# Retention then SwiGLU FFN on one core: FFN of the first chunk begun on two batches, with one more weight block loaded before the fourth batch

## The chip, the cores and the metric

The kernel runs on one core of a Trainium2 chip. The metric is the device time in microseconds from one launch to its end. The times of the kernel before are a median of 237.69 us over 7 runs, from 237.36 to 238.91. Five engines matter: TensorE (PE), VectorE (DVE), ScalarE (ACT), GpSimd (POOL) and the DMA queues, of which GpSimd issues most transfers and SyncE (SP) the first and the last.

## The reference

Inputs are q, k, v of shape (4 batches, 8 heads, 768 positions, 64), two FFN weights of 512 x 1536, one of 1536 x 512, and a gain vector. The first half is a recurrent retention per batch and head, the second an FFN over all 3072 tokens of width 512 (8 heads of 64):

```python
state = gamma[None, :, None, None] * state + np.einsum('bhd,bhe->bhde', k[:, :, t], v[:, :, t])
y[:, :, t] = scale * np.einsum('bhd,bhde->bhe', q[:, :, t], state)
...
xn = x / rms * rms_g
g = xn @ w_gate
silu = g * (1.0 / (1.0 + np.exp(-g)))
val = xn @ w_val
return (silu * val @ w_out)
```

## The kernel before, in words

The 768 positions are cut into six chunks of 128. A *group* is one chunk of all four batches, 512 token columns. For each group there is an attention part, batch by batch, and an FFN part over the 512 columns together. The recurrence is turned into matmuls within a chunk (scores with a decay mask) and a running state per batch between chunks.

The attention part is written as pieces, each named by a letter in the lists of the code. `piece_c` casts batch 0's first loads to bf16. `piece_v` (V) scales v by the decay into vp, on VectorE for batches 0 to 2 of chunk 0 and otherwise on GpSimd. `piece_t` (T) transposes q and k on TensorE for chunks 0 and 1, eight 128-wide matmuls and one ScalarE copy to qkT; for later chunks it issues DMA transposes from SyncE. `piece_a` (A) computes the scores, eight matmuls on 64 rows, and masks them with two VectorE multiplies into am. `piece_y` (Y) computes y, in chunks after the first also the part from the state and kv for the state's update, and ends with ScalarE's sum of squares (xsq). `piece_rstd` (R) makes the reciprocal root on GpSimd. `piece_n` (N) scales y to xn on VectorE. `piece_x` (X) transposes xn on TensorE and evicts it to the batch's 128 columns of xnT: for batches 0 and 1 of chunk 0 by four ScalarE activations, else by one VectorE multiply. `piece_s` and `piece_sb` (S) make the state of chunk 0: four matmuls, one ScalarE copy, two GpSimd casts.

The FFN part of a group has 12 blocks of 128 hidden units. Block n is `gv(n)` (L332 on): four matmuls for the gate (g_ps), four for the value (v_ps), each with the group's columns as the moving side, then silu on ScalarE (sg) and one multiply on VectorE (hT). The down projection follows: in group 0 in twelve pieces of four matmuls (three thirds of the hidden units by four batches), in later groups batch by batch. PSUM has two pools of four buffers, one for the FFN (fps) and one for attention (aps); Y of chunk 0 takes its buffer from the FFN's pool.

The order of all work is written out by hand, since the tile framework runs in manual order. Each engine takes its instructions strictly as they are written. The prologue is the string in L405 and L406: letters with a batch number, H with a count for warm-up matmuls of 256 columns on zeros, G and U for one piece of gate and value weights. After it the main loop (L426 on) goes through the *slots* of a group: each slot is one FFN block or one down piece, followed by pieces of the next chunk's attention, placed by PLAN1 for chunk 1 and PLAN for later ones, and by loads and early pieces for the chunk after that (AHEAD0, AHEAD, LATE0; L is a load of q, k and v, W one of w_out). In group 0, slots 0 to 3 use columns of three batches only (`gv_first`), X of batch 3 stands in slot 1, and the fourth batch's columns of these four blocks follow in slot 3, packed as 128-wide matmuls into one PSUM bank.

All loads by GpSimd go through one queue in the order of issue. The framework turns over eight semaphores for them, so that each issue waits for the landing of the eighth before it, and the instructions behind it on GpSimd wait too. In the prologue the order is q, k, v of batches 1 to 3, then three pairs of weight pieces: 384, 384 and 768 hidden units (WB, L142).

Of the kernel before, what the change touches and what calls it, by code (L numbers as in the profile page):

```python
# [9 lines left out]
F32 = mybir.dt.float32  # L10
BF16 = mybir.dt.bfloat16
# [6 lines left out]
def kernel(  # L18
# [11 lines left out]
    nc = tc.nc  # L30
    ctx.enter_context(tc.manual_schedule())

    B, H, S, D = q.shape
    C = 128
# [27 lines left out]
            nc.sync.dma_start(out=x, in_=src[0].rearrange("h (c p) d -> c p h d", p=C)[0])  # L62
            raw[name] = x

    def load(c, b):
        d = cur.setdefault((c, b), {})
        for name, src in (("qb", q), ("kb", k)):
            x = work.tile([128, DM], BF16, name=name, bufs=8)
            nc.gpsimd.dma_start(  # L69
                out=x.rearrange("p (h d) -> p h d", h=H),  # L70
                in_=src[b].rearrange("h (c p) d -> c p h d", p=C)[c])
            d[name] = x
        d["v_f"] = loads.tile([128, H, D], F32, name="v_f")
        nc.gpsimd.dma_start(out=d["v_f"], in_=v[b].rearrange("h (c p) d -> c p h d", p=C)[c])  # L74

    cur = {}
    load_first()
# [42 lines left out]
    nc.vector.memset(mhalf, -0.5)  # L120
    ident = const.tile([128, 128], BF16, name="ident")
    make_identity(nc, ident)
    for b in range(1, B):
        load(0, b)

    g_bc = const.tile([128, DM], F32, name="g_bc")
# [12 lines left out]
    wg_v = moe_w_gate.rearrange("(k p) n -> p k n", p=128)  # L139
    wv_v = moe_w_val.rearrange("(k p) n -> p k n", p=128)  # L140
    wo_v = moe_w_out.rearrange("(n p) m -> p n m", p=128)
    WB = ((0, 384), (384, 768), (768, DFF))  # L142

    def load_wg(i):
        sl = slice(*WB[i])
        nc.gpsimd.dma_start(out=wg_b[:, :, sl], in_=wg_v[:, :, sl])

    def load_wv(i):
        sl = slice(*WB[i])
        nc.gpsimd.dma_start(out=wv_b[:, :, sl], in_=wv_v[:, :, sl])  # L150
# [65 lines left out]

    def piece_y(c, b):
        d = cur[c, b]
        pool, tag = (fps, "ff") if c == 0 else (aps, "at")
        y_ps = pool.tile([128, H, D], F32, name="y_ps", tag=tag)  # L220
        first = True
        for hp in range(NHP):
            for i in range(2):
                h = 2 * hp + i
                last = c == 0 and h == H - 1
                nc.tensor.matmul(y_ps[:, h, :], d["am"][:, i, hp, :], d["vp"][:, h, :],  # L226
                                 start=first, stop=last, skip_group_check=True)
                first = False
        if c > 0:
            for hp in range(NHP):  # L230
                nc.tensor.matmul(y_ps[:, 2 * hp:2 * hp + 2, :], d["qT"][:, hp, :], st_b[b][:, hp, :],  # L231
                                 start=False, stop=hp == NHP - 1, skip_group_check=True)
        if 0 < c < NCH - 1:
            kv_ps = piece_kv(c, b)
        x = y_ps if c == 0 else work.tile([128, H, D], F32, name="x", bufs=5)
        if c > 0:
            nc.vector.tensor_tensor(  # L237
                out=x, in0=y_ps, in1=ydec[:, c, :, None].to_broadcast([128, H, D]), op=ALU.mult)
        xsq = work.tile([128, DM], F32, name="xsq", bufs=1)
        ssq = work.tile([128, 1], F32, name="ssq")  # L240
        nc.scalar.activation(xsq, x.rearrange("p h d -> p (h d)"), AF.Square,  # L241
                             accum_out=ssq)
        d["ssq"] = ssq
        d["x"] = x
        if c == 0:
            return
        piece_rstd(c, b)
        if c < NCH - 1:
            nc.vector.tensor_tensor(out=st_f[b], in0=st_f[b], in1=kv_ps, op=ALU.add)
            piece_sb(b)  # L250

    def piece_kv(c, b):
        d = cur[c, b]
        kv_ps = aps.tile([128, NHP, 128], F32, name="kv_ps", tag="at")
        for hp in range(NHP):
            sl = slice(hp * 128, (hp + 1) * 128)
            nc.tensor.matmul(kv_ps[:, hp, :], d["kb"][:, sl],  # L257
                             d["vp"][:, 2 * hp:2 * hp + 2, :], start=True, stop=True)
        return kv_ps

    def piece_s(b):
        nc.scalar.copy(st_f[b], piece_kv(0, b))

    def piece_sb(b):
        for i in range(2):
            r = slice(i * 64, i * 64 + 64)
            nc.gpsimd.tensor_copy(st_b[b][r, :, i * 64:i * 64 + 64], st_f[b][r, :, i * 64:i * 64 + 64])  # L267
# [21 lines left out]
    def piece_x(c, b):  # L289
        d = cur[c, b] if c == 0 else cur.pop((c, b))  # L290
        if c > 1:
            return
        xn = d["xn"]
        xt_ps = aps.tile([128, KS, 128], BF16, name="xt_ps", tag="at")
        for s in range(KS):
            nc.tensor.transpose(xt_ps[:, s, :], xn[:, s * 128:(s + 1) * 128], ident)  # L296
        xnT = cur[c, "xnT"][:, :, b * C:(b + 1) * C]
        if c == 0 and b < 2:
            for s in range(KS):
                nc.scalar.activation(xnT[:, s, :], xt_ps[:, s, :], AF.Copy, scale=g_col[:, s:s + 1])  # L300
            return
        nc.vector.tensor_tensor(
            out=xnT, in0=xt_ps,
            in1=g_col[:, :, None].to_broadcast([128, KS, 128]), op=ALU.mult)
# [5 lines left out]

    PLAN = dict(a=(5, 5, 9, 9), y=(7, 8, 11, 12), n=(9, 10, 13, 13))

    PLAN1 = dict(v=(7, 9, 11, 14), t=(8, 10, 12, 15), a=(9, 11, 14, 17), y=(10, 13, 16, 19), n=(12, 15, 18, 21), x=(13, 17, 20, 22))

    def attention(c):
        s = [[] for _ in range(24 if c == 1 else 16)]
        s[0].append(lambda: begin(c))
        plan = PLAN1 if c == 1 else PLAN
        pieces = dict(v=piece_v, t=piece_t, a=piece_a, y=piece_y, n=piece_n, x=piece_x)
        for b in range(B):  # L320
            for n, slot in plan.items():
                s[slot[b]].append(lambda f=pieces[n], b=b: f(c, b))
        return s


    def ffn(c):
# [5 lines left out]
        def gv(n0, n1=None, t=slice(0, GT)):  # L332
            n1 = n0 + 1 if n1 is None else n1
            w = t.stop - t.start
            g_ps = fps.tile([128, n1 - n0, w], F32, name="g_ps", tag="ff")
            v_ps = fps.tile([128, n1 - n0, w], F32, name="v_ps", tag="ff")
            for ps, w_b in ((g_ps, wg_b), (v_ps, wv_b)):
                for n in range(n0, n1):
                    for s in range(KS):
                        nc.tensor.matmul(ps[:, n - n0, :], w_b[:, s, n * 128:(n + 1) * 128], xnT[:, s, t],  # L340
                                         start=s == 0, stop=s == KS - 1)
            sg = ffw.tile([128, n1 - n0, w], BF16, name="sg")
            nc.scalar.activation(sg, g_ps, AF.Silu)  # L343
            nc.vector.tensor_tensor(out=hT[:, n0:n1, t], in0=sg, in1=v_ps, op=ALU.mult)  # L344


        EARLY = 4
        early = slice(0, GT - C)

        def gv_first(n):  # L350
            gv(n, t=early)
            if n == 1:
                piece_x(0, B - 1)
            if n == EARLY - 1:
                gv(0, EARLY, slice(GT - C, GT))

        o_t = {}

# [22 lines left out]
            nc.sync.dma_start(out=out_v[c, b], in_=o_sb)  # L381

        for n in range(NFF):
            slots.append(lambda n=n: gv_first(n) if c == 0 and n < EARLY else gv(n))
        if c == 0:
            for i in range(3):
                for b in range(B):
# [11 lines left out]
    def warm_up(c, n):  # L399
        for i in range(n):  # L400
            nc.tensor.matmul(hot_ps, hot[:, 0:128], hot, start=True, stop=True)  # L401

    P = dict(C=lambda c, b: piece_c(b), V=piece_v, T=piece_t, A=piece_a, Y=piece_y,
             R=piece_rstd, N=piece_n, X=piece_x, G=lambda c, i: load_wg(i), U=lambda c, i: load_wv(i), H=warm_up)
    for step in ("H9 H8 C0 T0 H4 V0 A0 H4 V1 T1 H4 G0 Y0 R0 U0 H4 A1 V2 T2 H4 Y1 R1 G1 U1 H2 A2 N0 T3 Y2 R2 "  # L405
                 "X0 N1 H2 A3 X1 N2 H9 H6 X2 H3 V3 Y3 H6 G2 U2 R3 N3").split():  # L406
        P[step[0]](0, int(step[1]))
    make_causal()
    load(1, 0)

    L, T, V, W = load, piece_t, piece_v, lambda c, i: load_wo(i)
    AHEAD = {1: ((L, 0),), 3: ((L, 1),), 5: ((L, 2),), 7: ((T, 0),), 8: ((T, 1),), 9: ((L, 3),), 11: ((T, 2),),
             13: ((V, 0),), 14: ((V, 1), (T, 3)), 15: ((V, 2), (V, 3))}


    AHEAD0 = {2: ((L, -1, 1),), 4: ((W, 0),), 5: ((L, -1, 2),), 6: ((W, 1),), 8: ((L, -1, 3),), 9: ((W, 2), (L, 0)),
              11: ((L, 1),), 13: ((T, 0),), 14: ((L, 2),), 15: ((T, 1),), 19: ((T, 2), (L, 3))}
    LATE0 = {0: ((V, 0), (V, 1), (V, 2)), 1: ((T, 3),), 4: ((V, 3),)}

    def ahead(c, i):  # L420
# [5 lines left out]
    for c in range(NCH):  # L426
        f_slots = ffn(c)
        a_slots = attention(c + 1) if c + 1 < NCH else [[] for _ in range(16)]
        for i, f_slot in enumerate(f_slots):
            if i == NFF + 1 and c > 0:  # L430

                for f in a_slots[i]:
                    f()
                a_slots[i] = []
            f_slot()
            if c == 0 and i < B:
                piece_s(i)
                piece_sb(i)
            for f in a_slots[i]:
                f()  # L440
            ahead(c, i)
            if c == 0 and i == 22:
                nc.sync.dma_start(out=g_bc, in_=moe_rms_g.partition_broadcast(128))
# [28 lines left out]
```

## Time and profile before

| What | Value |
|---|---|
| median of 7 runs | 237.69 us |
| the profiled execution | 237.69 us |
| its span, first to last instruction | 236.0 us |
| TensorE busy | 226.5 us |
| VectorE, ScalarE, GpSimd busy | 126.8, 88.9, 128.6 us |
| first FFN matmul starts at | 20.29 us |
| first down matmul starts at | 45.02 us |
| first FFN matmul of group 1 starts at | 61.53 us |
| landing of k and v of batch 3, chunk 0 | 14.63, 15.76 us |
| landing of the weight pairs (gate, value) | 17.25, 19.89; 21.81, 23.73; 27.48, 31.45 us |

In the lines of the profile, L and a number is the line of the kernel, then come engine, operation and the tiles written and read. In the timeline the first two columns are start and duration in us; in the chain of work too. Square brackets give the idle time before an instruction and what ended it. TensorE's matmuls overlap and their ends are modelled, so the distance from start to start is the better measure of one. Letters with a number (Y3, X2) stand for a piece and a batch; for chunk 1 a 1 stands in front (A11 is A of batch 1 in chunk 1).

### The profile page before, as it was taken

The numbers are of one execution on the slowest core, as the hardware profiler recorded it, in microseconds if no ns is written. First come the engines' busy times: TensorE is split into PE (matmuls) and PEld (weight loads), VectorE is DVE, ScalarE is ACT, GpSimd is POOL, SyncE is SP. The second block draws the span as 40 slices with busy tenths as digits, with TensorE's granted clock in tenths as the row PEclk, the third lists the DMA queues.
The fourth block names the chain that finished last, engine by engine and source line by source line (L and its number), as shares of the span: only waits on it lengthen the run. The fifth ranks groups of instructions, "written<-read, shape, count | busy, mean of one in ns | idle before, by whom it ended". The sixth has DMA issues, their size and how long they took to land.

```text
span 236.0 us, 4231 instructions
## 1 busy us (share of the span) xinstructions
PE 226.5 (96%) x1587; PEld 119.3 (51%) x1613; DVE 126.8 (54%) x212; ACT 88.9 (38%) x172; POOL 128.6 (55%) x198
## 2 busy tenths in 40 slices
PE   7979999999899999999999999999999999999994
PEld 4657744565345555445554445554445554444443
DVE  6585435678347794147794147794148582243300
ACT  7475534432433433333433333433332532433221
POOL 8978989987997458970559970559300202000000
PEclk9999999999999999999999999999999999999999
DMA  8999999999999999999698999295900025200022
GB/s 140 176 191 205 211 192 205 208 194 130 190 278 178 116 161 158 178 188 99 94 128 120 171 215 141 34 132 136 181 0 0 3 44 150 75 0 0 0 89 90
DMA packets 87956, 30.69 MB, mean 130 GB/s; under 512 B 78528, under 2 KB 83392, under 8 KB 87936
## 3 DMA queue, kind: packets, MB, share of 16 engines
q0 software_dynamic: 54432, 16.78, 74.5%
q1 hardware_dynamic: 32832, 13.51, 29.7%
q8 instruction: 12, 0.20, 0.4%
q10 hardware_dynamic: 672, 0.13, 0.3%
q14 instruction: 8, 0.07, 0.1%
HBM read 28.58 MB, written 6.29 MB: 148 GB/s over the span
## 4 chain that ended last, share of the span: by engine, by line
PE 85%; DVE 4%; ACT 4%; POOL 3%; issue 2%; ACTq 0%; DVEq 0%; POOLq 0%
PE g_ps L340 26%; PE v_ps L340 26%; PE o_ps L375 21%; PE a_ps L208 3%; PE y_ps L226 2%; PE hot_ps L401 2%; PE y_ps L231 2%; PE kv_ps L257 2%; DVE am L214 1%; DVE xn L286 1%; PE o_ps L365 1%; ACT xsq L241 1%; DVE x L237 1%; PE xt_ps L296 1%; POOL rstd L274 1%
## 5 line engine op out<-in xcount | busy, mean ns | idle before, releaser
L344 DVE TENSOR_TENSOR hT<-sg,v_ps 128x512 bf16<-128x512 bf16 (+1 forms) x73 | 49.5, 678 | 80.0 <-PE v_ps L340 70.1
L340 PE MATMUL v_ps<-xnT,wv_b 128*128 128x512 bf16 (+2 forms) x298 | 73.5, 368 | 0.4
L340 PE MATMUL g_ps<-xnT,wg_b 128*128 128x512 bf16 (+2 forms) x293 | 73.2, 368 | 0.5
L343 ACT ACTIVATE sg<-g_ps 128x512 bf16<-128x512 f32 (+1 forms) x73 | 43.0, 589 | 64.9 <-PE g_ps L340 62.5
L375 PE MATMUL o_ps<-wo_b,hT 128*128 128x512 bf16 x267 | 61.9, 379 | 0.5 <-issue 0.2
L340 PEld LDWEIGHTS <-wv_b 128*128 128x128 bf16 x304 | 29.1, 98 | 33.1
L340 PEld LDWEIGHTS <-wg_b 128*128 128x128 bf16 x304 | 27.7, 98 | 29.4 <-issue 0.4
L375 PEld LDWEIGHTS <-hT 128*128 128x128 bf16 x276 | 26.2, 98 | 28.7 <-DVE hT L344 0.2
L271 POOL TENSOR_SCALAR ms<-ssq 128x1 f32<-128x1 f32 x24 | 5.6, 232 | 62.2 <-ACT xsq L241 62.0
L241 ACT ACTIVATE xsq<-x 128x512 f32<-128x512 f32 x20 | 12.6, 630 | 35.1 <-DVE x L237 33.3
L214 DVE TENSOR_TENSOR am<-a_ps,causal 128x512 bf16<-128x512 f32 x40 | 24.9, 679 | 0.0
L380 ACT COPY o_sb<-o_ps 128x512 f32<-128x512 f32 x23 | 13.2, 582 | 29.3 <-PE o_ps L375 23.3
L69 POOL DMA_DIRECT2D qb<-in_q_dram x23 | 21.9, 950 | 0.3 <-issue 0.2
L175 POOL TENSOR_TENSOR vp<-v_f,vdec 128x512 bf16<-128x512 f32 x21 | 21.5, 1041 | 0.5
L74 POOL DMA_DIRECT2D v_f<-in_v_dram x23 | 21.3, 925 | 0.1
L69 POOL DMA_DIRECT2D kb<-in_k_dram x23 | 20.8, 902 | 0.0
L267 POOL CAST st_b<-st_f 64x256 bf16<-64x256 f32 x40 | 18.1, 454 | 1.3
L237 DVE TENSOR_TENSOR x<-y_ps,ydec 128x512 f32<-128x512 f32 x20 | 13.7, 684 | 2.9 <-PE y_ps L231 2.9
L282 DVE SCALAR_TENSOR_TENSOR xn<-x,rstd,g_bc 128x512 bf16<-128x512 f32 x16 | 12.7, 791 | 3.5 <-POOL rstd L274 3.5
L274 POOL TENSOR_TENSOR rstd<-ms,mhalf 128x1 f32<-128x1 f32 x24 | 13.3, 555 | 2.0
L401 PE MATMUL hot_ps<-hot 128*128 128x256 bf16 x65 | 11.6, 329 | 1.1 <-DVE hot L93 1.1
L226 PEld LDWEIGHTS <-am 128*128 128x128 bf16 x192 | 8.8, 98 | 5.3 <-DVE am L214 0.9
(71 smaller groups left out, 145.3 us busy)
## 6 DMA issues: line engine op xcount, KB each, us to landing
v_f<-in_v_dram POOLq DMA_DIRECT2D x23, 256.0 KB, 7.5
out_dram<-o_sb SPq DMA_DIRECT2D x23, 256.0 KB, 2.4
qb<-in_q_dram POOLq DMA_DIRECT2D x23, 128.0 KB, 6.0
kb<-in_k_dram POOLq DMA_DIRECT2D x23, 128.0 KB, 7.1
wo_b<-in_moe_w_out_dram POOLq DMA_DIRECT2D x3, 512.0 KB, 9.6
wg_b<-in_moe_w_gate_dram POOLq DMA_DIRECT2D x2, 384.0 KB, 6.5
wv_b<-in_moe_w_val_dram POOLq DMA_DIRECT2D x2, 384.0 KB, 7.6
wg_b<-in_moe_w_gate_dram POOLq DMA_DIRECT2D x1, 768.0 KB, 8.9
```

The source lines that it names most:

```text
L69: nc.gpsimd.dma_start(out=x.rearrange("p (h d) -> p h d", h=H), in_=src[b].rearrange("h (c p) d -> c p h d", p=C)[c])
L74: nc.gpsimd.dma_start(out=d["v_f"], in_=v[b].rearrange("h (c p) d -> c p h d", p=C)[c])
L175: (nc.vector if c == 0 and b < 3 else nc.gpsimd).tensor_tensor(out=d["vp"], in0=d["v_f"], in1=vdec[:, c, :, None].to_broadcast([128, H, D] ...
L214: nc.vector.tensor_tensor(out=am[:, i], in0=a_ps[i], in1=mask, op=ALU.mult)
L237: nc.vector.tensor_tensor(out=x, in0=y_ps, in1=ydec[:, c, :, None].to_broadcast([128, H, D]), op=ALU.mult)
L267: nc.gpsimd.tensor_copy(st_b[b][r, :, i * 64:i * 64 + 64], st_f[b][r, :, i * 64:i * 64 + 64])
L274: nc.gpsimd.tensor_tensor(out=rstd, in0=ms, in1=mhalf, op=ALU.pow)
L340: nc.tensor.matmul(ps[:, n - n0, :], w_b[:, s, n * 128:(n + 1) * 128], xnT[:, s, t], start=s == 0, stop=s == KS - 1)
L343: nc.scalar.activation(sg, g_ps, AF.Silu)
L344: nc.vector.tensor_tensor(out=hT[:, n0:n1, t], in0=sg, in1=v_ps, op=ALU.mult)
L375: nc.tensor.matmul(o_ps, hT[:, n, b * C:(b + 1) * C], wo_b[:, n, :], start=n == 0, stop=n == NFF - 1)
L401: nc.tensor.matmul(hot_ps, hot[:, 0:128], hot, start=True, stop=True)
```

## The change

The weights' first dimension of the hidden units is cut into four equal pieces of 384. The prologue issues the first two pairs of weight pieces before the loads of q, k, v of batch 3, which are now issued one by one, and the other two pairs behind them. T, A, Y, R, N and X of batch 3, and X of batch 2, leave the prologue; V of batch 3 goes to GpSimd behind the first load of chunk 1. Batch 1's X is evicted by VectorE.

Group 0's first twelve slots are `first(i)`: slot 0 has blocks 0 and 1 on two batches together, X of batch 2, block 2 on two batches, and the third batch's columns of blocks 0 to 2 packed. Slots 1 to 7 have blocks 3 to 9 on three batches, each followed by pieces of the fourth batch and the states. Slots 8 to 10 have the fourth batch's columns of blocks 0 to 9, packed, then come blocks 10 and 11 on all columns. Group 1 begins with blocks 0 and 1 on three batches (`second`), with X of chunk 1's batch 3 between them. PLAN1 is shifted by one or two slots, and the loads of AHEAD0 with it; the first two loads of chunk 2 are both issued in slot 10.

```diff
-    WB = ((0, 384), (384, 768), (768, DFF))
+    WB = tuple((i * 384, (i + 1) * 384) for i in range(4))
...
-        pool, tag = (fps, "ff") if c == 0 else (aps, "at")
+        pool, tag = (fps, "ff") if c == 0 and b < B - 1 else (aps, "at")
...
-        if c == 0 and b < 2:
+        if (c, b) == (0, 0):
             for s in range(KS):
                 nc.scalar.activation(xnT[:, s, :], xt_ps[:, s, :], AF.Copy, scale=g_col[:, s:s + 1])
...
-    PLAN1 = dict(v=(7, 9, 11, 14), t=(8, 10, 12, 15), a=(9, 11, 14, 17), y=(10, 13, 16, 19), n=(12, 15, 18, 21), x=(13, 17, 20, 22))
+    PLAN1 = dict(v=(9, 10, 13, 16), t=(9, 11, 13, 16), a=(10, 12, 15, 18), y=(11, 14, 17, 20),
+                 n=(13, 16, 19, 22), x=(15, 18, 21, None))
...
-        def gv_first(n):
-            gv(n, t=early)
-            if n == 1:
-                piece_x(0, B - 1)
-            if n == EARLY - 1:
-                gv(0, EARLY, slice(GT - C, GT))
+        def first(i):
+            two, three, third, fourth = slice(0, 2 * C), slice(0, 3 * C), slice(2 * C, 3 * C), slice(3 * C, GT)
+            if i == 0:
+                gv(0, 2, two)
+                piece_x(0, 2)
+                gv(2, 3, two)
+                gv(0, 3, third)
+            elif i < 8:
+                gv(i + 2, t=three)
+            else:
+                gv(*((0, 4), (4, 8), (8, 10), (11, 12))[i - 8], fourth if i < 11 else slice(0, GT))
+                if i == 10:
+                    gv(10)
+            for f, *x in {1: ((piece_s, 0),), 2: ((piece_t, 0, 3), (piece_s, 1)), 3: ((piece_a, 0, 3),),
+                          4: ((piece_y, 0, 3), (piece_rstd, 0, 3), (piece_s, 2)), 5: ((piece_n, 0, 3), (piece_s, 3)),
+                          7: ((piece_x, 0, 3),)}.get(i, ()):
+                f(*x)
+
+        def second(n):
+            gv(n, t=slice(0, GT - C))
+            if n == 0:
+                piece_x(1, B - 1)
+            else:
+                gv(0, 2, slice(GT - C, GT))
...
-    for step in ("H9 H8 C0 T0 H4 V0 A0 H4 V1 T1 H4 G0 Y0 R0 U0 H4 A1 V2 T2 H4 Y1 R1 G1 U1 H2 A2 N0 T3 Y2 R2 "
-                 "X0 N1 H2 A3 X1 N2 H9 H6 X2 H3 V3 Y3 H6 G2 U2 R3 N3").split():
+    for step in ("H9 H8 C0 T0 H4 V0 A0 H4 V1 T1 H4 G0 U0 Y0 G1 U1 R0 H4 A1 V2 T2 H4 q3 Y1 R1 k3 H2 A2 H6 N0 Y2 R2 v3 "
+                 "H2 X0 N1 H3 X1 N2 H6 G2 U2 G3 U3").split():
...
-    AHEAD0 = {2: ((L, -1, 1),), 4: ((W, 0),), 5: ((L, -1, 2),), 6: ((W, 1),), 8: ((L, -1, 3),), 9: ((W, 2), (L, 0)),
-              11: ((L, 1),), 13: ((T, 0),), 14: ((L, 2),), 15: ((T, 1),), 19: ((T, 2), (L, 3))}
+    AHEAD0 = {3: ((L, -1, 1),), 5: ((W, 0),), 6: ((L, -1, 2),), 8: ((W, 1),), 9: ((L, -1, 3),),
+              10: ((W, 2), (L, 0), (L, 1)), 13: ((T, 0),), 15: ((T, 1),), 16: ((L, 2),), 20: ((L, 3),), 23: ((T, 2),)}
```

More of the change, by code (lines that the diff above doesn't have):

```diff
@@ L63, in load_first, with load @@
             raw[name] = x
-    def load(c, b):
+    def load(c, b, parts="qkv"):
         d = cur.setdefault((c, b), {})
[L67 to L74, printed above, removed]
+        for n in parts:
+            if n == "v":
+                x = d["v_f"] = loads.tile([128, H, D], F32, name="v_f")
+            else:
+                d[n + "b"] = work.tile([128, DM], BF16, name=n + "b", bufs=8)
+                x = d[n + "b"].rearrange("p (h d) -> p h d", h=H)
+            nc.gpsimd.dma_start(out=x, in_=dict(q=q, k=k, v=v)[n][b].rearrange("h (c p) d -> c p h d", p=C)[c])
     cur = {}
@@ L122 @@
     make_identity(nc, ident)
-    for b in range(1, B):
+    for b in (1, 2):
         load(0, b)
@@ L262, in piece_s @@
         nc.scalar.copy(st_f[b], piece_kv(0, b))
+        piece_sb(b)
     def piece_sb(b):
@@ L321, in attention @@
             for n, slot in plan.items():
-                s[slot[b]].append(lambda f=pieces[n], b=b: f(c, b))
+                if slot[b] is not None:
+                    s[slot[b]].append(lambda f=pieces[n], b=b: f(c, b))
         return s
@@ L344, in gv @@
             nc.vector.tensor_tensor(out=hT[:, n0:n1, t], in0=sg, in1=v_ps, op=ALU.mult)
-        EARLY = 4
-        early = slice(0, GT - C)
-        def gv_first(n):
-            gv(n, t=early)
-            if n == 1:
-                piece_x(0, B - 1)
-            if n == EARLY - 1:
-                gv(0, EARLY, slice(GT - C, GT))
+        def first(i):
[19 more added lines that the diff above has]
+                piece_x(1, B - 1)
+            else:
+                gv(0, 2, slice(GT - C, GT))
         o_t = {}
@@ L383, in ffn @@
         for n in range(NFF):
-            slots.append(lambda n=n: gv_first(n) if c == 0 and n < EARLY else gv(n))
+            slots.append(lambda n=n: first(n) if c == 0 else second(n) if c == 1 and n < 2 else gv(n))
         if c == 0:
@@ L403 @@
     P = dict(C=lambda c, b: piece_c(b), V=piece_v, T=piece_t, A=piece_a, Y=piece_y,
-             R=piece_rstd, N=piece_n, X=piece_x, G=lambda c, i: load_wg(i), U=lambda c, i: load_wv(i), H=warm_up)
-    for step in ("H9 H8 C0 T0 H4 V0 A0 H4 V1 T1 H4 G0 Y0 R0 U0 H4 A1 V2 T2 H4 Y1 R1 G1 U1 H2 A2 N0 T3 Y2 R2 "
-                 "X0 N1 H2 A3 X1 N2 H9 H6 X2 H3 V3 Y3 H6 G2 U2 R3 N3").split():
+             R=piece_rstd, N=piece_n, X=piece_x, G=lambda c, i: load_wg(i), U=lambda c, i: load_wv(i), H=warm_up,
+             **{n: lambda c, b, n=n: load(c, b, n) for n in "qkv"})
+    for step in ("H9 H8 C0 T0 H4 V0 A0 H4 V1 T1 H4 G0 U0 Y0 G1 U1 R0 H4 A1 V2 T2 H4 q3 Y1 R1 k3 H2 A2 H6 N0 Y2 R2 v3 "
+                 "H2 X0 N1 H3 X1 N2 H6 G2 U2 G3 U3").split():
         P[step[0]](0, int(step[1]))
@@ L409 @@
     load(1, 0)
+    piece_v(0, 3)
     L, T, V, W = load, piece_t, piece_v, lambda c, i: load_wo(i)
@@ L435 @@
             f_slot()
-            if c == 0 and i < B:
-                piece_s(i)
-                piece_sb(i)
             for f in a_slots[i]:
```

## The prediction

> **What bounds the kernel now.** I read the page first, then the chain that ended last, then the timeline by stretches. The page says that TensorE is busy almost throughout and holds most of that chain.
>
> ```profile
> PE 226.5 (96%) x1587; PEld 119.3 (51%) x1613; DVE 126.8 (54%) x212; ACT 88.9 (38%) x172; POOL 128.6 (55%) x198
> ...
> PE 85%; DVE 4%; ACT 4%; POOL 3%; issue 2%; ACTq 0%; DVEq 0%; POOLq 0%
> ```
>
> So time is won in two ways only: useful matmuls begin earlier, or TensorE waits less. It runs its list in order, so one late operand holds everything behind it. The timeline shows where useful work begins:
>
> ```profile
> 18.04 0.74 DVE L286 TENSOR_SCALAR xn<-y_ps,rstd 128x512 bf16<-128x512 f32 x1
> ...
> 19.28 0.69 DVE L302 TENSOR_TENSOR xnT<-xt_ps,g_col 128x512 bf16<-128x512 bf16 x1 [0.49 <-PE xt_ps L296]
> ...
> 19.63 0.82 PE L401 MATMUL hot_ps<-hot 128*128 128x256 bf16 x6
> ...
> 20.29 0.81 PE L340 MATMUL g_ps<-xnT,wg_b 128*128 128x384 bf16 x4
> ```
>
> The first FFN matmul waits for the third batch's columns (19.97), then for six warm-up matmuls. From there to group 1 TensorE waits, reckoned from start to start of its matmuls, about 1.9 us in all: 0.34 us (of a 0.44 us gap), 0.30 and 0.21 around the attention pieces, and 1.04 us at batch 3's last transpose, 59.31 to 60.35. After 66 us I find no wait worth a name.
>
> Two more stretches supply durations. First, a transpose followed by its eviction, with an hT multiply ahead of it on VectorE:
>
> ```profile
> 23.11 0.39 PE L296 MATMUL xt_ps<-ident,xn 128*128 128x128 bf16 x4
> ...
> 23.38 0.55 DVE L344 TENSOR_TENSOR hT<-sg,v_ps 128x384 bf16<-128x384 bf16 x1 [0.61 <-PE v_ps L340]
> 23.86 0.68 DVE L302 TENSOR_TENSOR xnT<-xt_ps,g_col 128x512 bf16<-128x512 bf16 x1
> ...
> 26.38 1.06 PE L340 MATMUL g_ps<-xnT,wg_b 128*128 128x128 bf16 x16
> 27.28 1.06 PE L340 MATMUL v_ps<-xnT,wv_b 128*128 128x128 bf16 x16
> ```
>
> From the transpose's start to usable columns it is 24.54 - 23.11 = 1.43 us. Second, in the chain of work, the chain from one batch's y to the next batch's scores:
>
> ```profile
> 42.32 0.61 DVE x L237
> ...
> 43.01 0.59 ACT xsq L241
> ...
> 43.64 0.99 ACT qkT L198
> ```
>
> y began at 41.36 and the scores at 44.69, so 3.33 us.
>
> **The change, part by part.** Prices on TensorE, from start to start in these rows: four 384-wide matmuls 0.65, four 512-wide 0.86, a 256-wide 0.109, a 128-wide 0.056 (16 in 0.90). VectorE follows the last matmul's issue by 0.27 us, ScalarE by 0.20; on VectorE starts lie 0.60 apart for 512 elements, 0.47 for 384.
>
> *Start.* Batch 3's T and A leave the prologue, and batch 1's columns go from ScalarE to VectorE. Up to batch 2's scores (13.42) nothing differs. VectorE then ends am at 15.14, xn0 at 15.80, xn1 at 16.46 as before; batch 1's transposes start at 16.52, and its columns are ready 0.22 + 0.22 + 0.69 later, at 17.65. ScalarE, free of the 1.01 us qkT copy, ends batch 0's four columns near 17.4. The first FFN matmul comes at 17.7 in place of 20.29: **-2.6 us**. Weights: v2 landed at 12.87, and a 384-column piece takes 1.9 us of the stream (21.81 to 23.73), so the first pair lands near 14.8 and 17.0, needed at 17.7 and 18.6.
>
> *Moved work.* T (0.45), A (0.42), Y (0.22) of batch 3 and X (0.22) of batch 2, once under the waits of the prologue, now stand between FFN blocks: **+1.3**.
>
> *Narrow blocks.* Columns stay the same, matmuls become more: group 0 was 32x0.1625 + 32x0.056 + 64x0.216 = 20.8 and becomes 24x0.109 + 104x0.056 + 56x0.1625 + 16x0.216 = 21.0; with group 1 **+0.2**. The evictions become 15 pairs of silu and multiply in place of 13; ScalarE and VectorE are half idle, so these cost only where a wait below names them. [...] The row here, with the same loads beside it, shows 0.90 us for 16; I take the row.
>
> *New waits, walked from 17.7.* (1) Blocks 0 and 1 on two batches (16 matmuls, 1.75) bring it to 19.46, where X2 stands; block 2 on two batches follows, and then the packed third-batch columns, which want xnT2. VectorE has first the 512-element hT (19.73), then xnT (20.33 to 21.02). TensorE, covered by 0.22 + 0.87, is free at 20.55: **0.5**. Every later block stands behind, and so all evictions come as much later. (2) Blocks 3, 4, 5 with S0, T3, S1 and A3 bring it to 27.6, block 6 to 28.9, then Y3. ScalarE takes T3's copy (from 25.9, 0.90), S1's copy (0.5), only then block 5's silu (27.3 to 27.8); VectorE takes block 5's hT, and only then batch 3's two am (28.3 to 29.6). Y3 starts at 29.6: **0.7**. Behind it S2 and block 7 wait, and from Y3 hangs xsq, rstd, xn (33.0), X3, which is not late for it. Its PSUM buffer comes from the pool of the attention pieces and was T3's, free since 26.9: no wait there. (3) Blocks 7, 8, 9 and S2, S3 end near 34.2; X3 follows, and directly behind it block 0 to 3 of the fourth batch, which need xnT3. The measured 1.43 + 0.06 less the transposes' own 0.22: **1.3**. Before, two 384-wide blocks stood between and hid it. Here nothing does; the whole fourth batch and, behind it, blocks 10 and 11 start later. (4) The fourth batch's columns, T10, blocks 10 and 11, A10: Y10 starts near 44.4 (wait 0.1). Then T11 and one down piece stand before A11: 0.67 + 0.45 + 0.87 = 2.0 against the 3.3 of the chain above (ScalarE's list has xsq ahead of T11's copy, as before): before, a full block (1.73) stood in place of the down piece, and the gap was 0.34. Now **1.3**, and every down piece of group 0 is behind it. (5) X10 to X12 have 2 slots more and wait for nothing; Y13 waits about **0.2** for its am behind other work on VectorE. Sum **+4.1**.
>
> *Waits that go.* Group 1 opens on three batches, 1.30 us of work before X13; its xn is ready near 62.3 against a start there of 63.3, so the 1.04 is gone. With the three smaller waits, which the list above replaces: **-1.9**.
>
> *Loads.* On GpSimd the first four weight pieces go ahead of q3, k3, v3, and the last two pieces are halved. The bytes before the next group's loads are the same, and the queue was full (pieces landed back to back up to 55 us). I get k3 22.6, v3 23.8, G2 25.7, U2 27.6, G3 29.6, U3 31.5, and after that the old times. U2 is needed at 28.2, U3 at 33.5. GpSimd's list is in order, and each issue waits for the landing of the eighth before it (the wo_b issue at 34.90 waited 0.39 for v_f). Batch 3's vp sits behind v10's issue, which waits for k3: done near 25.7, needed at 29.6. rstd of group 1's batch 0 sits behind both new loads of slot 10, done near 49.4; its xn runs after am at 49.4, its transpose at 51.8: hidden, with 2 us to spare. The wo pieces have 5 us.
>
> Sum: -2.6 + 1.3 + 0.2 + 4.1 - 1.9 = **+1.1 us**. The profiled execution took 237.69, with span 236.0, and is the median of the runs, so 237.1 for the span and **238.8 us**.
>
> **Rivals.** *A wash* (near 237.9): the waits are not additive, since a TensorE that is delayed once comes later to the next one; an early hold of 0.5 us (say U2) would be swallowed by Y3's wait. For it: (1) to (3) all hang on VectorE. Against: each is reckoned from the work just before it. *Faster* (near 236.3): one mechanism, shorter hand-over through VectorE and ScalarE. The price rests on 0.27 us and 0.60 us spacing; five waits at 0.5 us less would leave 1.6 of 4.1 and give -1.4. It decides when the new waits fall below 2.3 us. Against: all of these spacings recur over the whole trace. *Weights late* (near 240.5): U0 landed 2.64 us after G0, not 1.9. At that spacing for all six pieces up to U2, this lands some 4 us later, near 31.6; block 6 stands still for 3.4, and Y3's 0.7 is swallowed by that, so 2.7 more than forecast. I take two thirds of it, 1.7. It decides from 1.3 us of lateness on (0.6 of slack and those 0.7). Against: the four later spacings were 1.9. *The work is only moved* (start earlier, TensorE gap elsewhere) is the forecast itself.
>
> **How the numbers follow.** Forecast 0.55 with its own range 238.2 to 239.4; wash 0.22; faster 0.10; weights late 0.13. About 0.3% (0.7 us) is what a measurement of this kernel tells from no change. Faster is the third case, 0.10; within 0.3% is the wash and the low edge of the forecast, 0.28; slower the rest, 0.62. The range 237.2 to 240.2 leaves out most of the faster case and half of the late weights.
>
> **What would show it.** First FFN matmul at 17.7 (above 18.5: step one wrong). A gap before the packed third-batch matmuls (0.5), before batch 3's y (0.7), after the last transposes of group 0 (1.3, released by VectorE's xnT), and before the scores of group 1's batch 1 (1.3, released by ScalarE's qkT). No gap at X13. 128-wide matmuls at 0.9 us per 16. If the last two gaps are missing, the change is faster; if TensorE is found waiting for weights, slower than I say.

## The result, and the profile after

The changed kernel is slower: 239.51 us median against 237.70, a ratio of 1.007 with a 95% interval of 1.0052 to 1.0088, which is 1.2 to 2.1 us on 237.7. Its 15 timed runs lie from 238.26 to 243.16, and two more executions took 244.94 and 249.0. Of 36 runs of the kernel before, 31 lie within half a microsecond of their median; the longest took 242.81. All ratios leave out the runs that are more than 1.5% above the fastest of their kernel, most of them at a mean granted clock of 0.993 or lower, so for the changed kernel they leave out a part of what it costs.

The profiled execution of the changed kernel is the longest one, 249.0 us. Its page:

```profile
span 247.3 us, 4403 instructions
...
PE 227.3 (92%) x1667; PEld 122.8 (50%) x1692; DVE 128.2 (52%) x216; ACT 88.3 (36%) x171; POOL 129.5 (52%) x200
...
PEclk9999999999999999959999999999999999999999
...
PE 67%; DMA 13%; POOL 6%; DVE 4%; issue 4%; ACT 2%; SPq 2%; POOLq 0%; ACTq 0%; DVEq 0%
```

TensorE's busy time hardly changed, 227.3 against 226.5. What is new is 13% of the last chain on DMA and a slice with a lower clock, both in groups 1 and 2. The first 62 us are as a second trace of this kernel has them. Here is the timeline of that stretch:

```profile
17.57 1.03 PE L342 MATMUL g_ps<-xnT,wg_b 128*128 128x256 bf16 x8 [0.22 <-DVE xnT L302]
...
19.58 0.69 DVE L346 TENSOR_TENSOR hT<-sg,v_ps 128x512 bf16<-128x512 bf16 x1 [1.50 <-PE v_ps L342]
...
20.19 0.68 DVE L302 TENSOR_TENSOR xnT<-xt_ps,g_col 128x512 bf16<-128x512 bf16 x1
...
20.93 0.84 PE L342 MATMUL g_ps<-xnT,wg_b 128*128 128x128 bf16 x12 [0.36 <-DVE xnT L302]
```

```profile
27.68 0.55 DVE L346 TENSOR_TENSOR hT<-sg,v_ps 128x384 bf16<-128x384 bf16 x1 [1.75 <-ACT sg L345]
...
28.15 1.28 DVE L213 TENSOR_TENSOR am<-a_ps,cdec 128x512 bf16<-128x512 f32 x2
...
29.49 0.38 PE L225 MATMUL y_ps<-vp,am 128*128 128x64 bf16 x7 [0.40 <-DVE am L213]
...
34.05 0.39 PE L296 MATMUL xt_ps<-ident,xn 128*128 128x128 bf16 x4
...
34.79 0.68 DVE L302 TENSOR_TENSOR xnT<-xt_ps,g_col 128x512 bf16<-128x512 bf16 x1
...
35.53 0.68 PE L342 MATMUL g_ps<-xnT,wg_b 128*128 128x128 bf16 x9 [1.10 <-DVE xnT L302]
```

```profile
44.34 0.43 PE L225 MATMUL y_ps<-vp,am 128*128 128x64 bf16 x8
...
45.22 0.68 DVE L236 TENSOR_TENSOR x<-y_ps,ydec 128x512 f32<-128x512 f32 x1
...
46.30 0.63 ACT L240 ACTIVATE xsq<-x 128x512 f32<-128x512 f32 x1 [2.02 <-DVE x L236]
...
46.93 0.99 ACT L197 COPY qkT<-qk_ps 128x1024 bf16<-128x1024 bf16 x1
...
47.98 0.40 PE L207 MATMUL a_ps<-qkT 64*128 64x128 bf16 x8 [1.66 <-ACT qkT L197]
```

The useful work begins at 17.57. Then TensorE stops four times, at the four places of the forecast: before the packed third-batch columns, before batch 3's y, after the last transposes, and before the scores of chunk 1's batch 1. Each time the bracket names the engine that the forecast named. From start to start of its matmuls these waits are 0.52, 0.65, 1.26 and 1.51 us. The first three brackets are shorter, since ends of matmuls are modelled. The fourth is longer, since one matmul's record is missing: the down piece at 45.50 has four matmuls, of which the trace shows three. Without a wait, as in the version below with the loads spread, the scores begin 0.96 us after that piece; here they begin 2.47 after it.

The part that was not forecast lies in group 1. First TensorE's timeline, then the chain of work that led there:

```profile
81.93 0.40 PE L207 MATMUL a_ps<-qT,kT 64*128 64x128 bf16 x8
84.85 0.40 PE L207 MATMUL a_ps<-qT,kT 64*128 64x128 bf16 x8 [2.51 <-DMA kT<-kb]
```

```profile
63.16 0.89 POOL qb L73
64.05 10.39 DMA kb<-in_k_dram
...
74.46 10.34 DMA kT<-kb
...
84.85 0.40 PE a_ps L207 x8
```

The load of k for chunk 2's batch 3 takes 10.39 us to land and its DMA transpose 10.34, and TensorE waits 2.7 us for it, from start to start, at that batch's scores. In the kernel before, the same load was issued at 61.44 and landed at 67.25, the transpose was issued at 67.42 and landed at 75.33, and the scores came at 81.16, in one row with those of batch 2. Its trace has for the load, the transpose and the scores:

```profile
DMA to landing us min/median/max: 5.8/5.8/5.8
...
DMA to landing us min/median/max: 7.9/7.9/7.9
...
80.92 0.62 PE L208 MATMUL a_ps<-qT,kT 64*128 64x128 bf16 x16
```

So 5.8 us of slack became a wait. In this execution a second one follows, 5.5 us at the start of group 2 (105.85), where the last DMA transpose of xn lands at 105.76.

### The profile page after: what moved, and what is told of

Read it like the earlier page. It is cut to its first block, busy times and chain, and to the rows that moved or that the text cites. A ratio compares the mean times of both kernels' runs of the same rounds, so it can differ in the third digit from the quotient of the medians.

```text
span 247.3 us, 4403 instructions
## 1 busy us (share of the span) xinstructions
PE 227.3 (92%) x1667; PEld 122.8 (50%) x1692; DVE 128.2 (52%) x216; ACT 88.3 (36%) x171; POOL 129.5 (52%) x200
## 4 chain that ended last, share of the span: by engine, by line
PE 67%; DMA 13%; POOL 6%; DVE 4%; issue 4%; ACT 2%; SPq 2%; POOLq 0%; ACTq 0%; DVEq 0%
PE g_ps L342 22%; PE v_ps L342 21%; PE o_ps L393 16%; DMA kb<-in_k_dram 6%; DMA kT<-kb 4%; DMA xnT<-xn 3%; PE a_ps L207 2%; SPq L182 2%; POOL qb L73 1%; PE y_ps L225 1%; PE y_ps L230 1%; ACT xsq L240 1%; DVE hT L346 1%; PE o_ps L383 1%; DVE x L236 1%
## 5 line engine op out<-in xcount | busy, mean ns | idle before, releaser
L346 DVE TENSOR_TENSOR hT<-sg,v_ps 128x512 bf16<-128x512 bf16 (+2 forms) x76 | 49.9, 657 | 85.4 <-PE v_ps L342 72.7
L342 PE MATMUL g_ps<-xnT,wg_b 128*128 128x512 bf16 (+3 forms) x338 | 75.4, 347 | 7.5 <-issue 5.3
L342 PE MATMUL v_ps<-xnT,wv_b 128*128 128x512 bf16 (+3 forms) x343 | 75.0, 345 | 0.3
L345 ACT ACTIVATE sg<-g_ps 128x512 bf16<-128x512 f32 (+2 forms) x76 | 43.5, 573 | 79.1 <-PE g_ps L342 73.3
L342 PEld LDWEIGHTS <-wg_b 128*128 128x128 bf16 x348 | 30.3, 99 | 35.6 <-issue 7.9
L342 PEld LDWEIGHTS <-wv_b 128*128 128x128 bf16 x348 | 32.0, 99 | 31.7 <-issue 1.6
L282 DVE SCALAR_TENSOR_TENSOR xn<-x,rstd,g_bc 128x512 bf16<-128x512 f32 x16 | 13.2, 827 | 7.7 <-DMA xnT<-xn 4.9
L248 DVE TENSOR_TENSOR st_f<-st_f,kv_ps 128x512 f32<-128x512 f32 x16 | 10.8, 676 | 0.0
```

## The experiments

Theory A is the forecast: the loss is the sum of TensorE's waits in group 0. Theory B came with the result: about half of the loss is those waits, the rest is TensorE waiting in group 1 for transposes of chunk 2, by an amount that differs from run to run. The rival to both is the wash: waits taken out or put in are swallowed by the next ones. In the diffs, minus is the changed kernel (or, where said, the kernel before).

### The changed kernel again

No edit.

> The changed kernel as it is, again, for a second trace. Theory A (only the walked waits of group 0): runs close together near 238.8. Theory B (walked waits plus transposes of chunk 2 that come late by an amount that differs): the fastest runs at 238.3 to 238.7, others 1 to 4 us above them, and the gap at the scores of chunk 2's batch 3 again in a slower one.

242.29 us median (238.35 to 243.99). Its trace shows the same four waits (0.52, 0.65, 1.26, 1.51) to 0.02 us, and then 3.94 us at the scores of chunk 2's batch 3, where k took 11.1 us to land and kT landed at 86.04. No wait at group 2 this time. So what differs between the two traces is in group 1 and later, as B says; the first 62 us do not.

### The loads of chunk 2 where they were

```diff
-              10: ((W, 2), (L, 0), (L, 1)), 13: ((T, 0),), 15: ((T, 1),), 16: ((L, 2),), 20: ((L, 3),), 23: ((T, 2),)}
+              10: ((W, 2), (L, 0)), 11: ((L, 1),), 13: ((T, 0),), 14: ((L, 2),), 15: ((T, 1),), 19: ((T, 2), (L, 3))}
```

> The changed kernel with one part undone: the loads and transposes of chunk 2 go back to the slots of the kernel before (first loads of batches 0 and 1 in slots 10 and 11, third load in 14, fourth in 19, the transposes of batch 2 in 19 in place of 23). Theory A: the loss is the sum of the waits that the prediction walked in group 0, and the loads of chunk 2 add nothing; then 239.0 to 239.5, as the changed kernel. Theory B: some 0.9 us of the loss are those waits and the rest, which differs from run to run, is TensorE waiting in group 1 for the transposes of chunk 2's last batch; then 238.3 to 238.7 with runs no more than 0.6 us apart, and no gap at the scores of chunk 2's last batches.

239.17 us, from 239.02 to 239.53; ratio to the kernel before 1.0058 (1.0045 to 1.0070). In six runs the spread went, as B says (of 24 executions of the changed kernel 15 lie above 239.3): k took 6.7 us, kT landed at 74.12, 8.8 us ahead of its use. The level is the one that A named, but for another reason: a new wait of 0.73 us stands at the transposes of chunk 1's batch 3. The load now stands in slot 19, ahead of that batch's y in slot 20, so GpSimd issues it before the batch's rstd. Less this wait it is 238.4, inside B's range.

### Only the transposes of chunk 2's batch 2 earlier

```diff
-              ... 16: ((L, 2),), 20: ((L, 3),), 23: ((T, 2),)}
+              ... 16: ((L, 2),), 19: ((T, 2),), 20: ((L, 3),)}
```

> The changed kernel with one thing moved: the DMA transposes of chunk 2's batch 2 go to the queue of SyncE in slot 19, before the outputs and the last load, not in slot 23 behind them. Theory B, in the form that these transposes, late and side by side with the last load, hold up that load and the next transposes: 238.3 to 238.7 with runs within 0.6 us, no gap at chunk 2's last scores. Rival: what counts is that the third and fourth loads of chunk 2 are issued a slot or two later than before; then the spread of the changed kernel stays, with a median of 239 or more.

238.48 us, from 238.24 to 238.90; ratio 1.0032 (1.0021 to 1.0043), so +0.5 to +1.0 us. With one piece moved the spread is gone in these six runs, and the scores of batches 2 and 3 run together without a gap:

```profile
82.14 0.62 PE L207 MATMUL a_ps<-qT,kT 64*128 64x128 bf16 x16
```

In this trace the last matmul ends at 233.62, against 232.52 before: +1.1 us, and TensorE's only waits after its start are the four of group 0. In the changed kernel these transposes are queued on SyncE behind four outputs and the gain vector, and come to lie beside the load of k (issued at 63.71 and 65.09, landed at 72.63 and 76.17); here they are done at 64.45. What became shorter is above all the transpose of batch 3's k behind them, 7.1 us for 10.3; the load of k itself still took 9.1.

### The same transposes late, in the kernel before

```diff
-              11: ((L, 1),), 13: ((T, 0),), 14: ((L, 2),), 15: ((T, 1),), 19: ((T, 2), (L, 3))}
+              11: ((L, 1),), 13: ((T, 0),), 14: ((L, 2),), 15: ((T, 1),), 19: ((L, 3),), 23: ((T, 2),)}
```

> The kernel before with one thing moved: the transposes of chunk 2's batch 2 issued from slot 23 and not 19, behind the outputs and beside the fourth load. Theory B: this alone brings the late landing (k of batch 3 takes 10 us or more to land in place of 5.8, kT of batch 3 lands after 82 us in place of 75.3): fastest runs 237.4 to 237.9, others 1 to 5 us above. If the lateness comes from the other shifts of the changed kernel: 237.5 to 238.2 with no spread.

237.65 us, from 237.31 to 238.66; ratio 0.9997 (0.9982 to 1.0012). B's strong form falls. k took 7.8 us in place of 5.8, and kT landed at 76.26, but its use is at 80.97: the slack of the kernel before carries it. So the late transposes alone do not make the wait; together with the later load of the changed kernel they do.

### The last transposes of group 0 one slot earlier

```diff
-                          7: ((piece_x, 0, 3),)}.get(i, ()):
+                          6: ((piece_x, 0, 3),)}.get(i, ()):
```

> The changed kernel with the last transposes of group 0 (X of batch 3) one slot earlier, so that one block on three batches stands between them and the packed columns of the fourth batch. The prediction's third wait says that 1.26 us of TensorE's time go, less about 0.3 because xn3 is hardly ready: 0.9 to 1.3 us faster than the changed kernel. The rival, that TensorE's waits in group 0 are swallowed by later ones (wash), says 0 to 0.3 us.

On the changed kernel as it is, nearly all runs were long (241.6 us median, lowest 237.08), so that no ratio can be given. The same edit with the transposes of chunk 2's batch 2 in slot 19:

> The changed kernel with the transposes of chunk 2's batch 2 in slot 19, where the spread is gone (238.5), and X of batch 3 one slot earlier. The prediction's third wait (1.26 in the trace) less 0.3 for xn3: 237.2 to 237.6. Wash: 238.1 to 238.5.

237.45 us (lowest 237.08, three runs from 238.4 to 239.7, one of 252.03); ratio to the kernel before 0.9993 (0.9969 to 1.0017), against 1.0032 without the edit: 0.0039, about 0.9 us, from medians 1.03. The wait of 1.26 is gone from the trace, with a block of 1.30 us standing in its place. The forecast's third wait is real and is not swallowed. But moving the transposes of chunk 2's batch 2 does not rule out long runs.

### T of chunk 1's batch 1 one slot earlier

```diff
-    PLAN1 = dict(v=(9, 10, 13, 16), t=(9, 11, 13, 16), ...
+    PLAN1 = dict(v=(9, 10, 13, 16), t=(9, 10, 13, 16), ...
```

> The changed kernel with the transposes of chunk 1's batch 1 one slot earlier, ahead of batch 0's y, so that ScalarE copies them before it has the sum of squares of batch 0. The prediction's fourth wait (1.3 forecast, 1.7 in the trace of the changed kernel) should go: 1.3 to 1.7 us faster than the changed kernel. The rival, that the later chain of batch 1 takes it back (its y waits for am, its transposes for xn), says 0 to 0.6.

The lowest run is 236.72, 1.54 below the lowest of the changed kernel, so the wait of 1.51 can be gained whole. The ratio, 1.0004 (0.9980 to 1.0028), is 1.6 us below the changed kernel's, but 8 of 14 runs are long (median 241.73); the profiled one of these was held up at the same scores, by 4.6 us. An earlier TensorE meets a late kT sooner.

### The two halves of the change alone

First half: prologue, weight pieces and group 0's first twelve slots as changed, PLAN1, AHEAD0 and group 1 as before.

```diff
-            slots.append(lambda n=n: first(n) if c == 0 else second(n) if c == 1 and n < 2 else gv(n))
+            slots.append(lambda n=n: first(n) if c == 0 else gv(n))
...
```

> The first half of the change alone: prologue, weight pieces and group 0's first twelve slots as changed; attention slots, loads and start of group 1 as in the kernel before. The prediction's terms for it are -2.6 (start) + 1.3 (moved work) + 0.2 (narrow blocks) + 2.5 (waits 1 to 3), so +1.4: 238.8 to 239.4, with waits 0.5, 0.7 and 1.3 in the trace and 1.0 at the last transposes of chunk 1 as before. The rival (waits not additive, wash): 237.5 to 238.2.

238.67 us, from 238.66 to 239.12; ratio 1.0042 (1.0029 to 1.0055), so +0.7 to +1.3 for a forecast of +1.4, just below it. The waits in its trace are 0.52, 0.65, 1.26, and 1.04 at chunk 1's last transposes. The start is earlier by 2.4 us in this trace (17.86), and still the half loses.

Second half: the kernel before, with group 1 begun on three batches.

```diff
-    ... x=(13, 17, 20, 22))
+    ... x=(13, 17, 20, None))
...
+        def second(n):
+            gv(n, t=early)
+            if n == 0:
+                piece_x(1, B - 1)
+            else:
+                gv(0, 2, slice(GT - C, GT))
...
```

> The kernel before with one part of the change alone: group 1 begins on three batches, and the last transposes of chunk 1 stand after its first block. The prediction counts the wait of 1.04 us at those transposes as gained whole, less 0.03 for 16 more matmuls: 236.6 to 236.8. If the wait only moves (the packed columns of the fourth batch then wait for their eviction), 237.3 to 237.7.

236.16 us, from 235.99 to 237.24; ratio 0.9943 (0.9924 to 0.9963), 0.9 to 1.8 us faster than the kernel before. The 1.0 expected lies in this interval, though the median is below the range given for it. TensorE's timeline at the start of group 1:

```profile
57.83 2.32 PE L383 MATMUL o_ps<-wo_b,hT 128*128 128x512 bf16 x10
59.99 0.81 PE L341 MATMUL g_ps<-xnT,wg_b 128*128 128x384 bf16 x4
60.64 0.81 PE L341 MATMUL v_ps<-xnT,wv_b 128*128 128x384 bf16 x4
61.29 0.39 PE L296 MATMUL xt_ps<-ident,xn 128*128 128x128 bf16 x4
61.52 0.81 PE L341 MATMUL g_ps<-xnT,wg_b 128*128 128x384 bf16 x4
```

No gap is left, and the packed columns do not wait either. This half alone beats both kernels; the first half takes it away.

### Waits 2 to 4 removed

T and A of batch 3 earlier (wait 2), X earlier (wait 3), T of chunk 1's batch 1 earlier (wait 4), transposes of chunk 2's batch 2 in slot 19. Wait 1 stays.

```diff
-            for f, *x in {1: ((piece_s, 0),), 2: ((piece_t, 0, 3), (piece_s, 1)), 3: ((piece_a, 0, 3),),
+            for f, *x in {1: ((piece_s, 0), (piece_t, 0, 3)), 2: ((piece_s, 1), (piece_a, 0, 3)),
...
-                          7: ((piece_x, 0, 3),)}.get(i, ()):
+                          6: ((piece_x, 0, 3),)}.get(i, ()):
...
```

> The changed kernel with its named waits taken away one by one: T of batch 3 a slot earlier and A two thirds of a slot earlier (wait 2, 0.65 us), X of batch 3 one slot earlier (wait 3, 1.26 less 0.3), T of chunk 1's batch 1 one slot earlier (wait 4, 1.7 us), transposes of chunk 2's batch 2 in slot 19 (late loads). If the waits of the prediction add up: 238.4 - 0.65 - 0.95 - 1.6 = 235.2, so 235.0 to 235.6 and faster than the kernel before. If removed waits come back elsewhere: 236.5 or more.

236.68 us, lowest 236.09, and again 5 of 22 runs from 242.29 to 245.97; ratio 0.9955 (0.9937 to 0.9973). The waits do not add up to the 235.0 to 235.6 expected: 2, 3 and 4 are gone from the trace, but 0.87 us came back at the transposes of chunk 1's batch 0:

```profile
47.45 0.90 POOL L73 DMA_DIRECT2D v_f<-in_v_dram  x1
...
48.69 0.56 POOL L274 TENSOR_TENSOR rstd<-ms,mhalf 128x1 f32<-128x1 f32 x1
...
49.29 0.60 DVE L286 TENSOR_SCALAR xn<-x,rstd 128x512 bf16<-128x512 f32 x1 [2.55 <-POOL rstd L274]
...
49.94 0.40 PE L296 MATMUL xt_ps<-ident,xn 128*128 128x128 bf16 x4 [0.70 <-DVE xn L286]
```

This is the queue that the prediction had found hidden with 2 us to spare: GpSimd's rstd behind both loads of slot 10. With TensorE earlier by the removed waits, the spare time is used up. So I spread the loads:

```diff
-              10: ((W, 2), (L, 0), (L, 1)), 13: ((T, 0),), 15: ((T, 1),), 16: ((L, 2),), 19: ((T, 2),), 20: ((L, 3),)}
+              10: ((W, 2), (L, 0)), 11: ((L, 1),), 13: ((T, 0),), 14: ((L, 2),), 15: ((T, 1),), 19: ((T, 2),), 20: ((L, 3),)}
```

> The changed kernel with waits 2, 3 and 4 taken away as in the run that removed them together, and the loads of chunk 2 spread as in the kernel before (second in slot 11, third in 14), so that GpSimd's rstd of chunk 1's batch 0 no longer stands behind two of them. The wait of 0.87 at the transposes of that batch should go: 236.3 - 0.85 = 235.3 to 235.8, below both kernels, and the late runs of 242 to 246 should go. If the wait comes from the chain of y itself: 236.1 to 236.5. If the late runs have another cause, they stay.

236.22 us, from 236.10 to 236.37; ratio 0.9935 (0.9922 to 0.9948). The expected 235.3 to 235.8 was missed. The 0.87 went, and 1.18 us stand elsewhere, at y of chunk 1's batch 3:

```profile
54.51 0.92 POOL L73 DMA_DIRECT2D v_f<-in_v_dram  x1
...
55.49 1.04 POOL L174 TENSOR_TENSOR vp<-v_f,vdec 128x512 bf16<-128x512 f32 x1
...
56.58 0.39 PE L225 MATMUL y_ps<-vp,am 128*128 128x64 bf16 x8 [1.02 <-POOL vp L174]
```

GpSimd again: the batch's vp behind three issues of a load. Both kernels are beaten, but by no more than the second half alone beats them.

### The wait for the copy, in the second half

On the second half alone, T of chunk 1's batch 1 goes from slot 10 to slot 9 (minus is the second half alone).

```diff
-    ... t=(8, 10, 12, 15) ...
+    ... t=(8, 9, 12, 15) ...
```

> The kernel before with group 1 begun on three batches (236.2), and T of chunk 1's batch 1 one slot earlier, ahead of batch 0's y, which takes away the wait of 0.34 us for ScalarE's copy. If it adds up: 235.7 to 236.0. If batch 1's later pieces take it back: 236.1 to 236.4.

237.14 us, from 236.18 to 241.43; ratio 0.9966 (0.9942 to 0.9990). A miss: the wait of 0.34 went, the transposes of batch 0 wait 0.87 (0.30 before), and 5 of 22 runs take 240.2 to 241.4. kT of chunk 2's batch 3 landed at 79.32 for a use at 80.16.

### What the spread goes with

From the traces, for chunk 2's batch 3: how long k took to land, when kT landed, when its scores began, the time of the traced execution, and all executions.

| kernel | k, us | kT landed | scores | traced | lowest to highest, number |
|---|---|---|---|---|---|
| before | 5.8 | 75.33 | 81.16 | 237.69 | 237.30 to 242.83, 127 |
| before, late transposes | 7.8 | 76.26 | 80.97 | 237.57 | 237.31 to 238.66, 14 |
| first half alone | 7.9 | 78.25 | 82.89 | 239.12 | 238.66 to 239.12, 5 |
| second half alone | 8.6 | 76.98 | 79.87 | 236.08 | 235.99 to 237.24, 6 |
| changed, loads as before | 6.7 | 74.12 | 82.91 | 239.17 | 239.02 to 239.53, 6 |
| changed, transposes earlier | 9.1 | 80.56 | 82.37 | 238.59 | 238.24 to 238.90, 6 |
| the same, X earlier | 6.9 | 76.87 | 80.97 | 237.18 | 237.08 to 252.03, 14 |
| waits 2 to 4 removed, loads spread | 8.3 | 79.24 | 79.98 | 236.19 | 236.10 to 236.37, 6 |
| waits 2 to 4 removed | 7.4 | 79.33 | 80.34 | 236.56 | 236.09 to 245.97, 22 |
| second half, T earlier | 9.2 | 79.32 | 80.16 | 236.37 | 236.18 to 241.43, 22 |
| changed | 10.4 | 84.80 | 84.85 | 249.0 | 238.26 to 249.0, 17 |
| changed, again | 11.1 | 86.04 | 86.08 | 243.99 | 238.35 to 243.99, 7 |
| changed, X earlier | 11.1 | 83.82 | 83.86 | 241.78 | 237.08 to 244.38, 6 |
| changed, T earlier | 12.2 | 85.23 | 85.28 | 243.87 | 236.72 to 243.87, 14 |

In all four traces of long executions kT lands right before its scores; in all traces of short ones it lands 0.7 us or more ahead. So each long execution that was traced has this wait. But the slack of one traced execution does not say how far the others spread: the kernel before, with 5.8 us of slack in its trace, has 4 of 127 runs above 242, and the version with X earlier, with 4.1, has one of 252.03. Where those waited no trace shows. Why the landing differs between runs of one kernel stays open too: none of the traces shows what slows a load on a given pass.

## Why the prediction was right or wrong

The direction was right and the time, 239.51, lies in the range; the forecast of +1.1 us is close to what the mechanism that I described costs (+1.1 at the last matmul, +0.5 to +1.0 in the timed runs, once the late transposes are taken away). The measured +1.7 holds a second mechanism that I had not seen; that the time still lies in the range is owed to the width that I gave it for other reasons. Point by point:

- *Start*, -2.6: right. 17.57 for 17.7, released by VectorE's xnT, -2.7 in this trace. The first weight pair landed at 14.39 and 16.37 for 14.8 and 17.0.
- *Moved work* +1.3 and *narrow blocks* +0.2: no run measures them alone; 16 matmuls of 128 columns took 0.89 us (33.69 to 34.58 to 35.47 in the version with waits 2 to 4 removed and the loads spread), so 56 ns each, the price that the forecast had taken from the row of the kernel before (0.90 for 16).
- *New waits*: 0.52, 0.65 and 1.26 for 0.5, 0.7 and 1.3. Wait (4) was sized at 1.3 and measured 1.51, and the small waits of 0.1 before Y10 and 0.2 before Y13 did not come, so the new waits sum to 3.9 for a forecast of 4.1. In (4), from the end of x (45.90) ScalarE began its sum of squares only at 46.30, where the row that I had used shows 0.09 between the two. Why, the trace doesn't say.
- *Waits that go*: the 1.04 is gone in the changed kernel, and gained whole when done alone.
- *Loads* is the step that failed, in the words "and after that the old times", with "After 66 us I find no wait worth a name". I followed GpSimd's queue up to chunk 1 and stopped there. The fourth load of chunk 2 is issued 2.6 us later, the transposes of its batch 2 move past the outputs on SyncE's queue, and both then lie in the DMA queues side by side. kT came 9.5 us later than before; the slack was 5.8, and TensorE itself came 1.0 later, which leaves the wait of 2.7. I gave the moved T of slot 23 no line in the sum.
- Of the *rivals*, the wash is refuted by the edits that took out single waits: X earlier gained about 0.9 to 1.0 us of 1.26. In part it holds: of the 3.4 us of waits 2 to 4, taken out together, 0.9 to 1.2 came back at later places. The rival *weights late* did not occur; U2 landed at 27.06 for 27.6. *Faster* would have needed the two halves apart: the first loses 0.7 to 1.3 us by itself.

## What to carry to other kernels

An earlier start pays only where each later operand comes as much earlier: here 2.6 us gained were paid back by four hand-overs that had lost their cover, three of them readable beforehand to 0.1 us, and the fourth to 0.2, as the chain of two or three evictions less the matmuls between; and the pieces moved between the blocks add some 1.3 by the forecast's count. A piece that moves on a DMA queue has to be followed to the one that uses it last, with the slack at that point, since a slack of 6 us two stages on can be used up. Parts of a change should be timed alone: this one held a gain of 1.4 us that the other half hid.

## What the runs showed of the hardware that I had not expected

A late DMA can cost more than the wait. Two traces around a long wait, with the granted clock as the number before the DMA's share; first the wait of 5.5 us in the execution of 249.0 us, then one of 3.0 us in that with only the last transposes of group 0 moved:

```profile
100.55:103.96 3.41, 0.00 (x0) 0.00 (x0) 0.42 (x1) 0.58 (x1) 3.41 (x5) 1.00 1.00 117
...
105.85:110.78 4.93, 4.93 (x12) 1.78 (x13) 0.69 (x1) 0.60 (x1) 2.53 (x3) 0.50 1.76 201
```

```profile
81.03:84.44 3.41, 0.58 (x10) 0.36 (x11) 2.71 (x5) 0.18 (x1) 3.27 (x6) 1.00 2.03 107
84.44:87.85 3.41, 3.41 (x10) 1.21 (x9) 1.31 (x3) 0.60 (x1) 1.10 (x2) 0.50 1.62 169
```

After the wait TensorE runs at half clock: a 512-wide matmul takes 0.43 us in place of 0.22. The granted clock was 0.50 for 6.83 us in the execution of 249.0 us (103.96 to 110.78) and for 3.41 us in the other trace (84.44 to 87.85). In the execution of 249.0 us it had stood at 1.00 for 98.99 us before that, from 4.97 on, and stood there again for 136.53 us; measured in the 3.413 us that are half of 6.83, these are 29 and 40. In the trace of the kernel before it stood at 1.00 for 225.28 us, 66 of them. In the four traces that have a fall within the work, TensorE had been busy for little of the 3.41 us ahead of it: 0.00 (execution of 249.0 us), 0.58 (X earlier), 0.88 (T earlier) and 1.26 (changed, again). The first wait of the execution of 249.0 us, 2.7 us, lay across two stretches of that length, counted back from the fall at 103.96 (80.07 to 83.48 to 86.90), with 2.21 and 2.05 us of matmuls, and the clock stayed at 1.00. So in these traces the length of a wait alone does not tell whether the clock falls: it fell with up to 1.26 us of matmuls in such a stretch, and stayed with 2.05. What sets the length of the stretches no trace shows.

The price, as an estimate from these rows: half of 4.93 us, 2.5, on top of a wait of 5.5, and half of 3.41, 1.7, on top of one of 3.0. By the same rows 3.41 us of half clock in a span of 240 us make a mean clock of 0.993, and 6.83 make 0.986: these are the clocks of most of the long runs, also of three of the four of the kernel before (0.991 to 0.993; the fourth's is not on record).

The other surprise is how far a landing can stretch: k of chunk 2's batch 3 took from 5.8 (the kernel before) to 12.2 us (changed, T earlier) from issue to landing in these traces, and the DMA transpose of k behind it 7.9 in the kernel before and 10.3 in the execution of 249.0 us.
